# Query tiles by heads on the row halves: a recurrent-memory attention kernel on one Trainium2 core

## The chip, the cores and the metric

The kernel runs on one core of one Trainium2 chip. The metric is the device time in microseconds, the median of several runs. The engines are TensorE (PE, with its weight loads listed apart as PEld), VectorE (DVE), ScalarE (ACT), GpSimd (POOL) and SyncE (SP, which here only issues DMAs). ACT and POOL can issue DMAs too, each from its own queue. TensorE writes to PSUM, eight banks of 2 KB per partition, and DVE or ACT copy the results to SBUF.

## The reference

Two layers, each a segment-recurrent attention with memory followed by a gated feed-forward, both behind a layer norm and with a residual. The sequence has 2048 rows of 448, cut into 64 segments of 32; 8 memory rows go ahead of each segment, so L = 40.

```python
for s in range(n_seg):
    h = jnp.concatenate([mem, xs], axis=1)
    q = jnp.einsum('btd,dhe->bhte', h, Wq)
    k = jnp.einsum('btd,dhe->bhte', h, Wk)
    v = jnp.einsum('btd,dhe->bhte', h, Wv)
    scores = jnp.einsum('bhqe,bhke->bhqk', q, k) * scale
    scores = jnp.where(mask[None, None], scores, -1000000000.0)
    p = _softmax(scores, axis=-1)
    o = jnp.einsum('bhqk,bhke->bhqe', p, v)
    o = jnp.einsum('bhte,hed->btd', o, Wo)
    mem = o[:, :M, :].copy()
    outs.append(o[:, M:, :])
...
x = x + _A_ref(_layernorm(x), ...)
x = x + _B_ref(_layernorm(x), ...)
x = x + _A_ref(_layernorm(x), ...)
x = x + _B_ref(_layernorm(x), ...)
```

There are 16 heads of 256. `_B_ref` is `(relu(x Wg) * (x Wu)) Wd` with an inner width of 1792. The same weights serve both layers.

## The kernel before, in words

**Folding.** The kernel never forms q, k or v. For each head it prepares A = Wq Wk^T (448 x 448) and B = Wv Wo (448 x 448) once, from the weights. Then scores are (h A) h^T, and the output is the sum over heads of (p h) B. Dimension 448 is held in four chunks: three of 128 (kd 0 to 2) and a last one of 64 (kd 3). Heads go in pairs (index eo), four pairs (p4) make a half (hf), and there are two halves.

**Preparation, the A loop** (lines 374 to 409, eight head pairs p). `load_nat` (line 302) loads a pair's columns of Wq and Wk into one of six `nat` buffers by three DMAs on SP's queue; the 64 last rows lie in chunk 3, and the upper 64 partitions of it hold other rows (Wv's last rows beside Wk's). `flips` (line 323) transposes them on TensorE, 16 transposes for Wq and 16 for Wk, and copies the results to `qT`, `kT` and (Wv's last rows) `v3`. A unit of the loop is one (kd, eo): two products of 384 columns into an `aps` bank and two of 64 columns into `mx_ps`. `share` (line 316) gives each copy from PSUM to DVE or ACT, whichever a small model of the two expects to be done first. The flips of the next pair are put between the units (line 400). For kd = 3 only 64 of the 128 rows exist in A_sb, and the copies (lines 394 to 399) put some tiles on the lower and some on the upper 64 partitions, as the table `EARLY` wants it.

**Preparation, the B loop** (lines 411 to 437). Per pair six units of two products of 448 columns (`bps`), then a group of four half-width products (`v3` by `wo`), two on the left and two on the right column half of TensorE. Wv is flipped one pair ahead; Wo comes over POOL's queue, three ahead, each load held back by `spread` until TensorE has reached the place in the program.

**The order of work.** `in_order` chains all of TensorE's instructions in program order. `InOrder` does so for DVE and ACT, but only once `on` is set (line 1037), that is after the preparation; during it the compiler's scheduler may order the two engines' work. `bank` picks the PSUM bank that is free first by a running estimate. `keep_warm` issues products of zeros that nobody reads: eight ahead of the first transposes, four between the flips of the first Wq and the first Wk.

**The scan** (line 1039). 68 steps; two chains run side by side, the two layers, the second four segments behind the first, so eight steps have one chain and 60 have two. Every other step also holds a feed-forward block. In a step `project` multiplies A by the rows (tiles of 128 columns, collected in banks of up to six tiles as `BANKS` orders them) and the copies fill `TQ` (tiles 0 to 23) and `TZ` (tiles 24 to 27, the 64 last dimensions). `project_early` does the kd 3 part of two banks at once, on the two row halves of TensorE. `scores` multiplies `TQ` and `TZ` by the rows, chunk by chunk in the order `KD`: for the second half, all memory and own scores of the first three chunks of `KD`, then those of the last chunk. `weigh_m` and `weigh_x` multiply the transposed weights `PT` by the rows, and `project_out` multiplies by B.

**Where things lie, before.** Tile t of a half holds chunk kd = t // 8, head parity eo = t // 4 % 2, pair p4 = t % 4, and TQ's columns are in the order of the tiles. So the last bank (tiles 18 to 23) belongs to chunk 2, and the bank before it (12 to 17) finishes chunk 1.

Of the kernel before, what the change touches and what calls it, by code (L numbers as in the profile page):

```python
# [15 lines left out]
DM = 448  # L16
# [26 lines left out]
EARLY = (((0, 6), (12, 18)), ((0, 6), (12, 18)))  # L43


KD = (0, 1, 3, 2)
# [4 lines left out]
def upper(hf, t):  # L51

    return any(b <= t < b + 6 for _, b in EARLY[hf])


def tidx(kd, eo, p4):

    return kd * 8 + eo * 4 + p4 if kd < 3 else 24 + p4


def build_kernel(ctx, tc, A_x, A_mem0, A_Wq, A_Wk, A_Wv, A_Wo, B_W_gate, B_W_up, B_W_down, out,
# [31 lines left out]
    class InOrder:  # L93

        def __init__(self, eng):
            self.eng, self.last, self.on = eng, None, False

        def __getattr__(self, name):
            f = getattr(self.eng, name)

            def call(*a, **k):
                r = f(*a, **k)  # L102
                if self.on:
                    if self.last is not None:
                        tc.add_manual_dep(r.ins, self.last,
                                          mybir.DependencyInfo(mybir.DependencyClass.NoSync,
                                                               mybir.DependencyReason.DATA),
                                          reason="order of issue")
                    self.last = r.ins.name
                return r  # L110

            return call
# [55 lines left out]
    nc.sync.dma_start(xp[1][:], x_dram[0:128])  # L168
# [120 lines left out]
    with tc.tile_pool(name="pre", bufs=6) as pre:  # L289
# [3 lines left out]
        nats = []  # L293
        for i in range(6):
            t = pre.tile([P, 4, 512], BF, name=f"nat{i}", bufs=1)
            nats.append(t)
        nc.gpsimd.memset(A_sb[64:128, 3, :, 24:NT, :], 0.0)
        for t in TQ + TZ + PX + PM + YB:
            nc.gpsimd.memset(t[:], 0.0)
        nn = [0]  # L300

        def load_nat(src, p, eng):
            t = nats[nn[0] % 6]
            nn[0] += 1
            cols = slice(512 * p, 512 * (p + 1))
            eng.dma_start(t[:, 0:3, :], src[0:384, cols].rearrange("(k p) n -> p k n", p=P))
            if src is Wv:
                return t
            eng.dma_start(t[0:64, 3, :], src[384:448, cols])
            eng.dma_start(t[64:128, 3, :], (Wq if src is Wq else Wv)[384:448, cols])  # L310
            return t

# [3 lines left out]
        def share(dst, src, n, per):  # L316
            cost = {dve: 60 + n * per[0], act: 170 + n * per[1]}
            ends = {e: max(until[e], now[0]) + cost[e] for e in cost}
            eng = min(ends, key=ends.get)
            until[eng] = ends[eng]  # L320
            evac(eng, dst, src)

        def flips(src, p, name):
            nat = load_nat(src, p, nc.sync)
            o = pre.tile([P, 4, 512], BF, tag="tT", name=name, bufs=4)

            def half(e2):
                tp = bank([P, 2, 512], BF, "tpw")
                n = 3 if src is Wv else 4
                for kd in range(n):  # L330
                    for e in range(2):
                        tr(tp[:, e, kd * 128:(kd + 1) * 128],
                           nat[:, kd, (2 * e2 + e) * 128:(2 * e2 + e + 1) * 128], ident[:])
                n = DM if src is Wk else 128 * n
                share(o[:, 2 * e2:2 * e2 + 2, 0:n], tp[:, :, 0:n], 2 * n, (0.6, 0.82))
                if src is Wk:
                    share(v3[:, p, 2 * e2:2 * e2 + 2, :], tp[:, :, DM:512], 128, (0.6, 0.82))

            return o, [lambda: half(0), lambda: half(1)]

        def queue(p):
            if p < NP:
                qT, a = flips(Wq, p, "qT")
                kT, b = flips(Wk, p, "kT")
                return (qT, kT), a + b
            if p == NP:
                return flips(Wv, 0, "vT")
            return None, []
# [13 lines left out]
        keep_warm(8)  # L362
# [5 lines left out]

        ready, todo = queue(0)
        for k, u in enumerate(todo):  # L370
            if k == 2:
                keep_warm(4)
            u()
        for p in range(NP):
            hf, p4 = divmod(p, 4)
            qT, kT = ready
            ready, todo = queue(p + 1)
            mx_ps = bank([P, 4, 128], F32, "mxw")
            for kd in range(4):
                for eo in range(2):  # L380
                    aps = bank([P, 3, 128], F32, "aps")
                    for t in range(2):
                        e = 2 * eo + t
                        mm(aps[:, :, :], qT[:, e, kd * 128:(kd + 1) * 128],
                           kT[:, e, 0:384], start=(t == 0), stop=(t == 1))
                    for t in range(2):
                        e = 2 * eo + t
                        mm(mx_ps[:, kd, eo * 64:eo * 64 + 64], qT[:, e, kd * 128:(kd + 1) * 128],
                           kT[:, e, 384:448], start=(t == 0), stop=(t == 1))
                    t0 = eo * 4 + p4  # L390
                    if kd < 3:
                        share(A_sb[:, kd, hf, t0:t0 + 17:8, :], aps[:], 384, (1.28, 0.85))
                    else:
                        up = [t for t in range(3) if upper(hf, t0 + 8 * t)]
                        for rows, ts in ((slice(64, 128), up), (slice(0, 64), [t for t in range(3) if t not in up])):
                            if ts:
                                d = ts[1] - ts[0] if len(ts) > 1 else 1
                                share(A_sb[rows, 3, hf, t0 + 8 * ts[0]:t0 + 8 * ts[-1] + 1:8 * d, :],
                                      aps[rows, ts[0]:ts[-1] + 1:d, :], 128 * len(ts), (1.28, 0.85))
                    if todo and 2 * kd + eo in (0, 2, 4, 5):  # L400
                        todo.pop(0)()
            share(A_sb[:, 0:3, hf, 24 + p4, :], mx_ps[:, 0:3, :], 384, (1.28, 0.85))
            share(A_sb[0:64, 3, hf, 24 + p4, :], mx_ps[0:64, 3, :], 128, (1.28, 0.85))
            if p >= 5:
                load_wo(p - 5)
            if p == 1:
                xn0 = normed(row_stats(xp[1]))
            if p == 2:
                first_rows(xn0)

        for p in range(NP):
            hf, p4 = divmod(p, 4)
            vT = ready
            ready, todo = flips(Wv, p + 1, "vT") if p + 1 < NP else (None, [])
            wo = wos.pop(0)
            for eo in range(2):
                for kd in range(3):
# [6 lines left out]
                    if kd == 1 and todo:  # L424
                        todo.pop(0)()
            bps = bank([P, 512], F32, "bps")
            for t in range(2):
                for eo in range(2):
                    e = 2 * eo + t
                    mm(bps[64 * eo:64 * eo + 64, 0:DM], v3[:, p, e, :], wo[:, e, :],  # L430
                       start=(t == 0), stop=(t == 1), tile_position=(0, 64 * eo))
            share(B_sb[:, hf, 24 + p4, 0:DM], bps[:, 0:DM], DM, (1.28, 0.85))
# [175 lines left out]
    def tile_of(ps, hf, t, i, chains, hb, j, kds, first, last):  # L608

        n = L * len(chains)  # L610
        for kd in kds:
            mm(ps[:, i * n:(i + 1) * n], A_sb[:, kd, hf, t, :], moving(hb, j, kd, chains),
# [518 lines left out]
```

## Time and profile before

| | us |
|---|---|
| median of 3 runs (1569.27 to 1571.19) | 1570.5 |
| the profiled execution | 1569.33 |
| its span | 1567.5 |
| start to the first `aps` product | 9.55 |
| A loop, to the first `bps` product | 38.35 |
| B loop, to the first `prj` product | 27.68 |
| first `prj` product to the end | 1491.9 |

The span is the time from the first to the last instruction; the time of the execution has some 1.8 us around it. The three stretches ahead of the scan end where the first product of the next stage starts in the timeline. Of the work before the scan, the eight loads each of Wq, Wk, Wv and Wo bring 384 to 448 KB apiece, and the 64 last rows of Wq, Wk and Wv come in separate loads of 64 KB.

### The profile page before, as it was taken

To read this page: it belongs to the slowest core of one execution; us is meant where nothing else is said; L and a number is where in the kernel's file an instruction comes from. 1 tells how busy PE (TensorE), PEld (TensorE's weight loads), DVE (VectorE), ACT (ScalarE), POOL (GpSimd) and SP (SyncE) were. 2 spreads that over 40 slices of the span, in tenths; PEclk is the share of its full clock that TensorE was granted. 3 is DMA by queue.
4 is the path that set the end of the run, shared out by engine and by line. 5 is a ranking of instruction groups with operands and counts; after the bars stand their busy time and mean duration, and the time that the engine had idled before them with its cause. 6 is when DMAs were issued, how large, how long until landed. Compare 5 with 4: busy or idle time off the path is not lost.

```text
span 1567.5 us, 89355 instructions
## 1 busy us (share of the span) xinstructions
PE 1554.4 (99%) x40988; PEld 1442.9 (92%) x40988; DVE 1111.4 (71%) x3654; ACT 757.7 (48%) x2123; POOL 78.0 (5%) x174
## 2 busy tenths in 40 slices
PE   9999999999999999999999999999999999999998
PEld 6688999999999999999999999999999999999897
DVE  8756777777767777777677777667777776677765
ACT  5754444454444445544454455444544554445443
POOL 3200000000000000000000000000000000000000
PEclk9999999999999999999999999999999999999999
DMA  8630000000000000000000000000000000000000
GB/s 239 205 86 9 8 10 9 5 8 10 9 10 9 10 10 5 9 9 10 9 10 9 10 3 10 9 10 9 9 10 10 4 9 10 10 8 7 6 7 9
DMA packets 28233, 33.21 MB, mean 21 GB/s; under 512 B 4168, under 2 KB 26960, under 8 KB 27856
## 3 DMA queue, kind: packets, MB, share of 16 engines
q1 hardware_dynamic: 26608, 23.76, 5.4%
q8 instruction: 320, 5.24, 1.4%
q0 software_dynamic: 1088, 3.68, 0.7%
q14 instruction: 57, 0.47, 0.1%
q10 hardware_dynamic: 160, 0.06, 0.0%
HBM read 23.70 MB, written 1.84 MB: 16 GB/s over the span
## 4 chain that ended last, share of the span: by engine, by line
PE 98%; DVE 1%; issue 0%; DMA 0%; SPq 0%; ACT 0%; POOL 0%; POOLq 0%; DVEq 0%; ACTq 0%
PE prj L144 32%; PE ox L144 25%; PE gps L144 6%; PE ups L144 6%; PE dps L144 6%; PE o L144 5%; PE y L144 4%; PE Sx L144 3%; PE pps L152 2%; PE bps L144 1%; PE aps L144 1%; PE Sm L144 1%; PE tpw L152 1%; PE ya L144 1%; PE yb L144 1%; PE tps L152 1%
## 5 line engine op out<-in xcount | busy, mean ns | idle before, releaser
L144 PE MATMUL prj<-hT,A_sb 128*128 128x80 bf16 (+3 forms) x15232 | 550.5, 199 | 2.2 <-issue 1.3
L144 PEld LDWEIGHTS <-A_sb 128*128 128x128 bf16 (+1 forms) x15232 | 504.8, 99 | 22.6 <-issue 3.2
L144 PEld LDWEIGHTS <-B_sb 128*128 128x128 bf16 (+1 forms) x15008 | 489.4, 103 | 13.7 <-issue 0.8
L144 PE MATMUL ox<-Y,B_sb 128*128 128x80 bf16 (+2 forms) x11256 | 443.5, 200 | 1.4 <-issue 1.4
L102 ACT CAST TQ<-prj 128x480 bf16<-128x480 f32 (+1 forms) x380 | 184.1, 497 | 103.1 <-PE prj L144 91.2
L102 DVE CAST Y<-y 128x256 bf16<-128x256 f32 x376 | 151.3, 457 | 39.8 <-PE y L144 39.5
L102 ACT CAST Y<-y 128x512 bf16<-128x512 f32 (+2 forms) x392 | 137.1, 419 | 67.5 <-PE y L144 61.8
L102 ACT ACTIVATE se<-se 128x160 f32<-128x160 f32 (+2 forms) x270 | 81.6, 302 | 138.3 <-DVE se L102 131.8
L102 DVE CAST TQ<-prj 128x480 bf16<-128x480 f32 (+1 forms) x228 | 128.7, 573 | 8.8 <-PE prj L144 8.3
L144 PE MATMUL gps<-xT,Wg_sb 128*128 128x128 bf16 (+3 forms) x1904 | 128.6, 216 | 0.0
L144 PEld LDWEIGHTS <-Wu_sb 128*128 128x128 bf16 (+1 forms) x1904 | 104.9, 97 | 5.6 <-issue 0.2
L102 ACT COPY os<-o 64x16 f32<-64x16 f32 (+3 forms) x134 | 25.5, 191 | 171.7 <-PE o L144 170.1
L144 PE MATMUL ups<-xT,Wu_sb 128*128 128x128 bf16 (+3 forms) x1632 | 106.8, 216 | 0.5 <-DVE xT L102 0.5
L144 PEld LDWEIGHTS <-Wg_sb 128*128 128x128 bf16 (+1 forms) x1904 | 106.7, 97 | 0.5 <-issue 0.5
L144 PEld LDWEIGHTS <-hk 40*128 40x128 bf16 (+1 forms) x1950 | 98.9, 96 | 8.6 <-issue 1.4
L102 DVE SCALAR_TENSOR_TENSOR hh<-gps,ut 128x512 bf16<-128x512 f32 (+2 forms) x136 | 78.1, 595 | 34.6 <-ACT ut L102 21.6
L102 ACT CAST TZ<-prj 64x320 bf16<-64x320 f32 (+2 forms) x264 | 97.0, 377 | 8.2 <-DVE TZ L102 5.3
L144 PE MATMUL dps<-Wd_sb,hh 128*128 128x448 bf16 (+1 forms) x504 | 93.3, 342 | 0.8 <-DVE hh L102 0.8
L102 ACT COPY PT<-pps 128x256 bf16<-128x256 bf16 (+1 forms) x136 | 47.2, 347 | 96.5 <-PE pps L152 92.1
L102 DVE TENSOR_REDUCE ssum<-se 128x4 f32<-128x160 f32 (+2 forms) x270 | 72.9, 270 | 24.1 <-ACT se L102 24.0
L144 PEld LDWEIGHTS <-TQ 128*128 128x128 bf16 x1938 | 85.8, 97 | 1.5 <-ACT TQ L102 0.8
L144 PE MATMUL y<-PT,hk 40*128 40x256 bf16 (+1 forms) x1280 | 86.3, 249 | 0.6 <-ACT Y L102 0.6
(126 smaller groups left out, 1902.3 us busy)
## 6 DMA issues: line engine op xcount, KB each, us to landing
wo<-in_A_Wo_dram POOLq DMA_DIRECT2D x8, 448.0 KB, 5.0
nat<-in_A_Wq_dram SPq DMA_DIRECT2D x8, 384.0 KB, 5.0
nat<-in_A_Wk_dram SPq DMA_DIRECT2D x8, 384.0 KB, 4.9
nat<-in_A_Wv_dram SPq DMA_DIRECT2D x8, 384.0 KB, 4.5
xa<-in_A_x_dram SPq DMA_DIRECT2D x32, 56.0 KB, 2.3
xa<-xp SPq DMA_DIRECT2D x32, 56.0 KB, 1.9
xp<-in_A_x_dram SPq DMA_DIRECT2D x30, 56.0 KB, 2.4
out_dram<-xa SPq DMA_DIRECT2D x30, 56.0 KB, 2.3
```

The source lines that it names most:

```text
L102: r = f(*a, **k)
L144: in_order(nc.tensor.matmul(out, lhsT, rhs, **k))
L152: in_order(nc.tensor.transpose(out, src, idn))
```

## The change

The tiles of the queries are numbered anew. A bank of six tiles now holds one head parity (eo) and six of the twelve (chunk, pair) positions: banks 0 and 6 the positions 0 to 5, banks 12 and 18 the positions 6 to 11. In `A_sb` the kd 3 rows of the even heads lie on partitions 0 to 63 and those of the odd heads on 64 to 127, and `a_tile` turns a tile's number into its place there. In `TQ`, `TZ`, `PT` and the tiles of B the two parities alternate, 16 columns each. Chunk 0 is complete after bank 6; chunks 1 and 2 both need bank 18. `KD` becomes (0, 3, 1, 2), and the second half's scores take the first two chunks, then the other two.

In the preparation, the 64 last rows are loaded apart (`nats3`, Wq's and Wk's side by side, Wv's of two pairs side by side), flipped by four transposes (`flip_last`), and the kd 3 rows of A come from four half-width products of 448 columns (`by_heads`, `last_rows`). The groups of half-width products of two pairs stand next to each other: at the end of an even pair and the start of the odd one. The first loads are cut in two halves of 256 columns, Wq's on SP's and Wk's on ACT's queue; later loads are asked for two pairs ahead and held back by `spread`. Seven idle products instead of eight and four. The first layer norm and the first rows move from the A loop to the B loop, and the first load of x goes behind the first asks. DVE and ACT keep program order from the start.

```diff
-EARLY = (((0, 6), (12, 18)), ((0, 6), (12, 18)))
-KD = (0, 1, 3, 2)
+EARLY = ((0, 6), (12, 18))
+KD = (0, 3, 1, 2)
...
+def a_tile(t):
+    if t >= 24:
+        return t
+    u = t // 12 * 6 + t % 6
+    return 3 * (t // 6 % 2 * 4 + u % 4) + u // 4
 def tidx(kd, eo, p4):
-    return kd * 8 + eo * 4 + p4 if kd < 3 else 24 + p4
+    return kd * 8 + p4 * 2 + eo if kd < 3 else 24 + p4
...
-    nc.sync.dma_start(xp[1][:], x_dram[0:128])
+    nats = [pre.tile([P, 3, 512], BF, name=f"nat{i}", bufs=1) for i in range(6)]
+    nats3 = [pre.tile([P, 512], BF, name=f"natl{i}", bufs=1) for i in range(3)]
+    for e in range(2):
+        cols = slice(256 * e, 256 * e + 256)
+        for i, (eng, src) in enumerate(((nc.sync, Wq), (nc.scalar, Wk))):
+            eng.dma_start(nats[i][:, :, cols], rows3(src, cols))
+            if e == 0:
+                eng.dma_start(nats3[0][FR[i], :], src[384:448, 0:512])
...
+        def ask(p):
+            if p < NP:
+                q, r = load_nat(Wq, p)
+                spread(r)
+                asked[p] = ([q, load_nat(Wk, p)[0]], load_last(((Wq, p), (Wk, p))))
+            elif p < 2 * NP:
+                v, r = load_nat(Wv, p - NP)
+                spread(r)
+                asked[p] = (v, load_last(((Wv, p - NP), (Wv, p - NP + 1))) if p % 2 == 0 else None)
...
+        def flip(nat, e2, dst):
+            tp = bank([P, 2, 512], BF, "tpw")
+            for kd in range(3):
+                for e in range(2):
+                    tr(tp[:, e, kd * 128:(kd + 1) * 128],
+                       nat[:, kd, (2 * e2 + e) * 128:(2 * e2 + e + 1) * 128], ident[:])
+            share(dst, tp[:, :, 0:384], 768, (0.6, 0.82))
+        def flip_last(nat, dst):
+            tp = bank([P, 4, 128], BF, "tpl")
+            for e in range(4):
+                tr(tp[:, e, :], nat[:, e * 128:e * 128 + 128], ident[:])
+            share(dst, tp[:].rearrange("p e (i d) -> p e i d", i=2), 512, (0.6, 0.82))
...
-        keep_warm(8)
+        keep_warm(7)
...
+        def by_heads(ps, a, b, n):
+            for t in range(2):
+                for eo in range(2):
+                    mm(ps[FR[eo], 0:n], a(2 * eo + t), b(2 * eo + t), start=(t == 0), stop=(t == 1),
+                       tile_position=(0, 64 * eo))
+        def last_rows(qk, hf, p4):
+            ps = bank([P, DM], F32, "apl")
+            by_heads(ps, lambda e: qk[:, e, 0, 384:DM], lambda e: qk[:, e, 1, :], DM)
+            eng = one_of(900, (1.28, 0.85))
+            for eo in range(2):
+                t0 = 3 * (eo * 4 + p4)
+                evac(eng, A_sb[FR[eo], 3, hf, t0:t0 + 3, :], ps[FR[eo], 0:384])
+            for eo in range(2):
+                evac(eng, A_sb[FR[eo], 3, hf, 24 + p4, 64 * eo:64 * eo + 64], ps[FR[eo], 384:DM])
         ready, todo = queue(0)
-        for k, u in enumerate(todo):
-            if k == 2:
-                keep_warm(4)
-            u()
+        ask(1)
+        for _ in range(3):
+            todo.pop(0)()
         for p in range(NP):
-            qT, kT = ready
-            ready, todo = queue(p + 1)
+            qk = ready
+            ask(p + 2)
+            ready, us = queue(p + 1)
+            todo += us
+            if p == 0:
+                nc.sync.dma_start(xp[1][:], x_dram[0:128])
+            if p % 2:
+                last_rows(qk, hf, p4)
-            for kd in range(4):
-                for eo in range(2):
+            for eo in range(2):
+                for kd in range(3):
...
+            if p % 2 == 0:
+                last_rows(qk, hf, p4)
...
         for p in range(NP):
             vT = ready
-            ready, todo = flips(Wv, p + 1, "vT") if p + 1 < NP else (None, [])
+            ask(p + 2 + NP)
+            ready, todo = queue_v(p + 1) if p + 1 < NP else (None, [])
+            if p % 2:
+                last_out(p, wo)
...
+            if p % 2 == 0:
+                last_out(p, wo)
+            if p == 1:
+                xn0 = normed(row_stats(xp[1]))
+            if p == 2:
+                first_rows(xn0)
...
-                T = TQ[hf][:].rearrange("p g u w -> p g (u w)")[:, :, 16 * i0:16 * (i0 + k)]
+                u0, eo = i0 // 12 * 6, i0 // 6 % 2
+                T = TQ[hf][:].rearrange("p g u w -> p g (u w)").rearrange("p g (t e q) -> p t e g q", e=2, q=16)
+                T = T[:, u0:u0 + 6, eo]
...
-                mem(KD[:3])
-                own(KD[:3])
-                mem(KD[3:])
-                own(KD[3:])
+                mem(KD[:2])
+                own(KD[:2])
+                mem(KD[2:])
+                own(KD[2:])
...
-                mm(yb[:, 128:192], hk[:, 3 + eo, :], PT[:, 64 * eo:64 * eo + 64], start=(eo == 0), stop=(eo == 1))
+                mm(yb[:, 128:192], hk[:, 3 + eo, :], PT[:].rearrange("p (b o q) -> p b o q", o=2, q=16)[:, :, eo, :], start=(eo == 0), stop=(eo == 1))
...
-                       PT[rows, :].rearrange("p (e o w) -> p e o w", e=2, o=2)[:, :, eo, :],
+                       PT[rows, :].rearrange("p (e b o q) -> p e b o q", e=2, o=2, q=16)[:, :, :, eo, :],
...
-    dve.on = act.on = True
```

`last_out` is the B loop's group of half-width products, by `by_heads` as before.

## The prediction

> **What bounds the kernel now.** First the busy shares and the chain of waits on the page, then the windows cut at the three stages before the scan and the scan itself.
>
> ```profile
> PE 1554.4 (99%) x40988; PEld 1442.9 (92%) x40988; DVE 1111.4 (71%) x3654; ACT 757.7 (48%) x2123; POOL 78.0 (5%) x174
> ...
> PE 98%; DVE 1%; issue 0%; DMA 0%; SPq 0%; ACT 0%; POOL 0%; POOLq 0%; DVEq 0%; ACTq 0%
> ```
> ```profile
> 0.00:9.55 9.55, 7.55 (x45) 4.02 (x46) 4.47 (x20) 1.31 (x2) 8.76 (x17) 1.00 0.69 205
> 9.55:47.90 38.35, 38.35 (x501) 29.81 (x500) 34.69 (x75) 24.64 (x69) 7.30 (x14) 1.00 0.89 265
> 47.90:75.58 27.68, 27.68 (x215) 14.54 (x214) 21.77 (x38) 20.24 (x37) 9.61 (x11) 1.00 0.60 190
> ...
> 116.40:1490.00 1373.60, 1371.02 (x36782) 1293.98 (x36778) 982.86 (x3259) 657.31 (x1801) 48.92 (x124) 1.00 0.03 9
> ```
> After the window's bounds come its length and the busy times of PE, weight loads, DVE, ACT and POOL, then granted clock, DMA share and GB/s. TensorE sets the pace from 9.55 us on: the A loop (9.55 to 47.90), the B loop (to 75.58) and the scan. So an edit is worth what it takes from TensorE's stream, and a new wait costs its full length. In the A loop DVE (34.69) and ACT (24.64) together fill 77% of two engines, and the DMA engines 89%: both covers are thin.
>
> The paces of TensorE come from starts in the timeline, since a product's own duration holds its pipeline's latency.
>
> ```profile
> 10.51 0.49 PE L144 MATMUL aps<-kT,qT 128*128 128x384 bf16 x2
> 10.83 0.22 PE L144 MATMUL mxw<-kT,qT 128*128 128x64 bf16 x2
> ...
> 11.27 0.61 PE L152 MATMUL tpw<-ident,nat 128*128 128x128 bf16 x8
> 11.72 0.49 PE L144 MATMUL aps<-kT,qT 128*128 128x384 bf16 x2
> ```
> ```profile
> 50.46 0.54 PE L144 MATMUL bps<-wo,vT 128*128 128x448 bf16 x2
> 50.93 0.57 PE L144 MATMUL bps<-wo,v 128*64 128x448 bf16 x4
> 51.43 0.93 PE L144 MATMUL bps<-wo,vT 128*128 128x448 bf16 x4
> ```
> A unit of the A loop (two products of 384 columns, two of 64) takes 10.51 to 10.89 = 0.38 us; a transpose 0.45/8 = 0.056 us; two products of 448 columns 0.38 us too (52.54 to 53.67 holds six). The four half-width products of 448 columns start at 50.93 where full ones would end at 50.84, and give way at 51.43: 0.38 us of work, since the two column halves run side by side, and 0.19 us of switching, 0.57 in all.
>
> **The first products.**
>
> ```profile
> 1.18 3.59 PE L144 MATMUL junk<-still 128*128 128x512 bf16 x8 [1.18 <-DVE still L171]
> ...
> 4.92 1.89 PE L152 MATMUL tpw<-ident,nat 128*128 128x128 bf16 x16
> ...
> 6.49 0.26 PEld L144 LDWEIGHTS <-still 128*128 128x128 bf16 x2
> ...
> 9.55 0.49 PE L144 MATMUL aps<-kT,qT 128*128 128x384 bf16 x2 [0.27 <-DVE kT L102]
> ```
> The eighth idle product starts at 4.14, so one takes 0.43 us. The first 16 transposes fill 4.92 to 6.49, 0.098 us each against 0.056 later: TensorE runs at about half pace until some 6.5 us, though the granted clock reads 1.00. Then K's loads hold the rest until 9.55. After the change seven idle products end at 1.18 + 7 x 0.43 = 4.2. The first Q half is issued at about 0.7 in the place of xp, and one such load landed 3.7 us after its issue (1.17 to 4.91), so it is there at 4.4 at the latest. K's half comes over ACT's queue, which may first load its table (0.73 to 2.01). 16 transposes at 0.098 bring 5.8 to 6.0; the last-needed copy of 768 elements (0.56 on DVE, 0.80 on ACT) ends near 6.4, where aps begins: **-3.15 us**. Bounds: 5.8 (everything on DVE, loads early) and 7.5 (table first, 2.0 + 3.7 + 16 transposes), that is -3.75 to -2.05. Half pace may outlast 6.4: each us of it costs 0.5; I take +0.3, bounds 0 and 1.7.
>
> [...]
>
> **Work on TensorE in both loops.** Per head pair the A loop goes from eight units to six: 16 x 0.38 = -6.08 us over eight pairs. Transposes: Q and K 32 to 28 a pair, 16 of them (not 32) before the first unit, V's last rows 4 per two pairs, and the first rows moved from A to B; in the loops 328 before and 328 after: 0. Column-pair groups: eight of 0.57 before (all in B, 4.56); after, eight in A and eight in B, two and two adjacent (end of an even pair, start of the odd one), 2 x 0.38 + 0.19 = 0.95 per two, eight times 0.95 = 7.60: +3.04. Together **-3.04 us**. If adjacent groups switch in between all the same, they cost 16 x 0.57 and this is -1.52.
>
> **Copies.** Per pair, kd 3's four pieces of 64 rows and mxw's (0.26 to 0.43 each, 1.55 together) give way to two of 64x384 and two of 64x64 (1.4, from 0.48 for 384 and about 0.2 for the small ones); Q and K flips get shorter (0.674 and 0.625 to 0.558), v's two of 0.267 go, one of 512 elements (0.44, between 0.265 at 128 and 0.558 at 768) comes. 7.4 us per pair falls to 6.8, and the pair from 4.8 to 2.28 + 28 x 0.056 + 0.475 = 4.32: 79% of two engines. Eight banks cover it on average, not in the burst where two groups of copies (2.8 us) fall together; the odd pair's group also needs the last flip's copy, with 0.38 + 0.48 in between against 0.2 + 0.56 to 0.80. DVE and ACT now keep program order here, so the layer norm's wait for POOL (0.23 + 0.57) holds what is queued behind it. I take +0.8, bounds 0 and 2.5.
>
> **Loads two ahead.** Each ask waits for TensorE's last product at that point and brings 896 KB in four issues. In A the loop lasts 4.3 us; Q is needed 4.7 after the ask and K 5.4, and at the 265 to 300 GB/s of this stage both halves (768 KB, 2.6 to 2.9 us after some 1.8 of issue and latency) are there: 0. In B a V load shares the engines with a Wo load asked at the same time.
>
> ```profile
> DMA to landing us min/median/max: 3.7/4.5/6.1
> ```
> ```profile
> wo<-in_A_Wo_dram POOLq DMA_DIRECT2D x8, 448.0 KB, 5.0
> ```
> The first line is nat in the B loop's window. V is needed 3.54 + 0.38, or 0.86 in odd pairs, after its ask: 4.2 on average. At 4.5 the six loops with a Wo load wait 0.3 each (2.0), at the least row 3.7 nothing. Before, these loads queued behind one another; now each is alone on SP's ring, so I take 1.0, bounds 0 and 3.5. SP's xp and first-rows loads stand behind the asks; the first step needs them 30 us later.
>
> [...]
>
> **The scan.** The count of instructions stays; new tile indices alone, and POOL's zeroing of A_sb in two halves for one of 0.95 us (done by 6, read after 70), cost 0. Scores of half 1 need the last bank's copy for two of four chunks now, not one.
>
> ```profile
> 568.18 0.56 ACT L102 CAST TQ<-prj 128x480 bf16<-128x480 f32 x1 [0.36 <-PE prj L144]
> ...
> 568.52 0.13 PEld L144 LDWEIGHTS <-TQ 128*128 128x128 bf16 x2
> ...
> 568.93 0.21 PEld L144 LDWEIGHTS <-TQ 128*128 128x128 bf16 x5
> ```
> ```profile
> 1544.11 0.42 ACT L102 CAST TQ<-prj 128x48 bf16<-128x48 f32 x2 [0.25 <-PE prj L144]
> ...
> 1544.58 0.14 PEld L144 LDWEIGHTS <-TQ 128*128 128x128 bf16 x3 [0.20 <-ACT TQ L102]
> ```
> The second pair shows a real wait: copy ends 1544.53, load at 1544.58, so 0.05 us to pass on. The copy of the first ends 568.74, free at 568.79. Before, the late chunk comes after 15 products, at 568.94; after, behind 2 of 0.035 and 8 of 0.026, at 568.80. In the other kind of step (copy ending 460.65, first load 460.48) it is 460.76 against 460.70. So the wait just vanishes: 0, and each 0.01 us that the copy is later costs 0.3 to 0.6 us over the 60 steps with two chains. The copies write runs of 16 elements as before, at twice the step: 0. PT is now read as a moving operand in runs of 16. The nearest row is prj, two runs of 40: 67 products in 2.29 us, 34.2 ns for 80 columns, where unbroken operands go at 0.16 us for 384, 33.3 for 80, so a break costs at most 0.9 ns; 60 more breaks a step make at most 54 ns, 3.2 us over the scan. I take 0, the row's break being buried. Nothing gains here, since TensorE waits for nothing.
>
> **The sum.** -3.15 + 0.3 - 3.04 + 0.8 + 1.0 = -4.1 us on the profiled execution's 1569.3 (span 1567.5 and 1.8 around it): 1565.2. The median lies 1.2 above that execution: **1566.4 us**.
>
> **Rivals.** (a) The waits do not come: -3.15 - 3.04 = -6.2, **1564.3**. For: nothing waits in A now. Against: the thinner covers. (b) Loads and copies eat the gain, at their bounds 3.5 + 2.5 with the late half pace 1.7: +1.5, **1572**; half of that excess leaves 1569. For: DMA at 89%. Against: loads fall to 917 KB in 4.3 us, 213 GB/s. (c) The slower side: interleaved TQ writes make the scores of half 1 wait for the last copy at their first load. Place: 568.52 waits for 568.79, 0.27, and 460.48 for 460.70, 0.22; 30 of each are 15 us, **1581**. It decides from 0.068 us a step, which is 4.1 us. For: the ranges of the two head parities now interlace. Against: before, the copies already wrote three-level patterns that spanned all of TQ, and the first load did not wait.
>
> **Chances.** Forecast 0.60, (a) 0.11, (b) 0.16, (c) with smaller forms of the same wait 0.13. About 0.2%, 3.1 us, is what a measurement can tell. The forecast gives 0.47 faster and 0.13 same, (a) 0.11 faster, (b) 0.11 same and 0.05 slower, (c) 0.13 slower: 0.58, 0.24, 0.18. The range reaches from (a) with an early start, 1563, to (b) at its bound, 1572; the forecast's own is 1564 to 1569.
>
> **What would show it.** aps starting near 6.4; the A loop near 35.3 us and the B loop near 29; PEld idle on nat loads in B; no TensorE idle ahead of TQ loads in the scan, whose window from the first prj to the end stays at 1491.9 us. I am wrong if that window moves by more than 2 us, or if the loops together last over 66.

## The result and the profile after

| | before | after |
|---|---|---|
| median of 22 runs each, us | 1569.09 (1567.79 to 1572.14) | 1571.71 (1570.30 to 1576.13) |
| the profiled execution | 1569.33 | 1570.71 |
| its span | 1567.5 | 1568.9 |
| start to the first `aps` product | 9.55 | 6.48 |
| A loop | 38.35 | 39.42 |
| B loop | 27.68 | 32.20 |
| first `prj` product to the end | 1491.9 | 1490.8 |

The ratio after to before is 1.0017 (95% interval 1.0010 to 1.0023): a small loss, where a gain was forecast. The time lies in the range given (1563 to 1572), but the sign is the other one. That it does is in part luck: the three runs that the forecast started from had a median of 1570.5, 1.4 us above that of the 22, so the time is 5.3 us above the forecast, but the change 6.7 (+2.6 where -4.1 was forecast). By stage: the start gained 3.07 us as forecast, the loops, forecast at 35.3 and 29, took 39.42 and 32.20, together far over the 66 that the prediction named as its sign of being wrong, and the scan moved by 1.1.

First the busy times and the chain of waits, shares of the span by engine, on the page of the changed kernel.

```profile
PE 1550.2 (99%) x40935; PEld 1440.1 (92%) x40935; DVE 1108.2 (71%) x3649; ACT 760.6 (48%) x2116; POOL 78.3 (5%) x175
...
PE 97%; DMA 2%; DVE 1%; issue 0%; ACT 0%; POOL 0%; SPq 0%; POOLq 0%; DVEq 0%
```

TensorE is busy for 4.2 us less than before, yet the span is 1.4 longer: the work did go away. What is new is DMA with 2% of the chain. The windows, cut at the same four places (columns as in the prediction), say where:

```profile
0.00:6.48 6.48, 4.87 (x23) 2.48 (x24) 4.18 (x16) 1.65 (x2) 5.67 (x16) 1.00 0.62 171
6.48:45.90 39.42, 35.89 (x448) 26.56 (x448) 29.80 (x64) 27.13 (x63) 9.71 (x14) 1.00 0.72 220
45.90:78.10 32.20, 28.74 (x237) 15.89 (x237) 23.49 (x46) 20.53 (x37) 10.87 (x14) 1.00 0.68 219
116.40:1490.00 1373.60, 1371.97 (x36817) 1295.06 (x36814) 982.65 (x3258) 656.80 (x1796) 48.91 (x124) 1.00 0.03 9
```

The first two figures of a line are its length and PE's busy time. Before, both loops had no gap. Now TensorE stands idle for 39.42 - 35.89 = 3.53 us in A and 32.20 - 28.74 = 3.46 in B; its busy times, 35.89 and 28.74, are close to the 35.3 and 29 forecast for the loops as a whole. Nearly all of it is waits for weight loads (in the order of the loops: total, times, longest):

```profile
PE tpw L154 <- DMA nat<-in_A_Wq_dram: 3.4, 3, 2.4
PE tpw L154 <- DMA nat<-in_A_Wv_dram: 3.5, 3, 2.2
```

The share of the DMA engines in A *fell*, from 0.89 to 0.72: the loads are not too many, they come too late. The chain in order of time (start, length, what) names the loads:

```profile
5.22 5.82 DMA nat<-in_A_Wq_dram
11.09 0.51 PE tpw L154 x6
...
14.79 5.60 DMA nat<-in_A_Wq_dram
20.44 0.51 PE tpw L154 x6
...
24.62 4.85 DMA nat<-in_A_Wq_dram
29.53 0.51 PE tpw L154 x6
...
49.54 4.43 DMA nat<-in_A_Wv_dram
54.02 0.51 PE tpw L154 x6
...
65.85 6.25 DMA nat<-in_A_Wv_dram
72.15 0.51 PE tpw L154 x6
```

Five times the end hangs on a weight load from the moment SP issues it until the transposes that use it: 4.43 to 6.25 us. A pass without waits lasts about 4.5 us in A and 3.6 in B (the busy times over eight). And SP's own queue in the timeline (start, length, issues) shows what stands ahead of two of these five:

```profile
12.43 0.37 SPq L317 DMA_DIRECT2D nat<-in_A_Wk_dram  x1
12.95 0.47 SPq L324 DMA_DIRECT2D natl<-in_A_Wq_dram  x1
13.47 0.59 SPq L324 DMA_DIRECT2D natl<-in_A_Wk_dram  x1
14.16 0.54 SPq L317 DMA_DIRECT2D nat<-in_A_Wk_dram  x1
14.79 1.35 SPq L317 DMA_DIRECT2D nat<-in_A_Wq_dram  x1
...
61.56 1.36 SPq L242 DMA_DIRECT2D Wu_sb<-in_B_W_up_dram  x2
62.97 0.42 SPq L317 DMA_DIRECT2D nat<-in_A_Wv_dram  x1
65.01 0.80 SPq L242 DMA_DIRECT2D Wu_sb<-in_B_W_up_dram  x2
65.85 0.43 SPq L317 DMA_DIRECT2D nat<-in_A_Wv_dram  x1
```

`spread` holds only the Wq load of a pair. The pair's Wk load and last rows are not held, and the compiler issues them first, though the program asks for Wq ahead of them: the load needed first goes last. (Counted through, the last rows and the second Wk load of this fence already belong to the pair after.) In B two held pieces of W_up, asked at the end of the pass before, go ahead of the held Wv load.

The scan shows nothing new. The page has 1.6 us of idle ahead of all 1938 loads of TQ, against 1.5 before (busy, mean ns of one, then the idle ahead and what ended most of it):

```profile
L146 PEld LDWEIGHTS <-TQ 128*128 128x128 bf16 x1938 | 85.7, 97 | 1.6 <-ACT TQ L105 0.9
```

### The profile page after: what moved, and what is told of

The parts are those of the page before. It is cut to its first block, busy times and chain, and to the rows that moved or that the text cites. A ratio compares the mean times of both kernels' runs of the same rounds, so it can differ in the third digit from the quotient of the medians.

```text
span 1568.9 us, 89231 instructions
## 1 busy us (share of the span) xinstructions
PE 1550.2 (99%) x40935; PEld 1440.1 (92%) x40935; DVE 1108.2 (71%) x3649; ACT 760.6 (48%) x2116; POOL 78.3 (5%) x175
## 4 chain that ended last, share of the span: by engine, by line
PE 97%; DMA 2%; DVE 1%; issue 0%; ACT 0%; POOL 0%; SPq 0%; POOLq 0%; DVEq 0%
PE prj L146 32%; PE ox L146 25%; PE gps L146 6%; PE ups L146 6%; PE dps L146 5%; PE o L146 5%; PE y L146 4%; PE Sx L146 3%; PE pps L154 2%; PE Sm L146 1%; DMA nat<-in_A_Wq_dram 1%; PE ya L146 1%; PE bps L146 1%; PE yb L146 1%; PE tps L154 1%; PE kps L146 1%
## 5 line engine op out<-in xcount | busy, mean ns | idle before, releaser
L105 DVE SCALAR_TENSOR_TENSOR hh<-gps,ut 128x512 bf16<-128x512 f32 (+2 forms) x136 | 78.1, 595 | 37.5 <-ACT ut L105 21.7
```

## The experiments

Each was timed against the kernel before on the same chip (the first four against a median of 1569.69 us, the next four 1569.55, the following three 1568.83, the last 1568.47; 15 to 28 runs each). The theory going in: the holding back of loads, and the order on SP that comes with it, cost the gain. The rivals: the copies, the order of VectorE and ScalarE, or the column-pair groups. In the expectations "pair 2" means the second pair (`p` = 1), except in the last one, which counts as the code does, as all of them do for the pieces of W_up and W_gate.

**1. No holds on the weight loads (e1).** The loads go as soon as a buffer is free.

```diff
-                spread(r)        # in ask(), Wq
-                spread(r)        # in ask(), Wv
```

> The changed kernel, but no load of Wq, Wk or Wv is held back by TensorE's progress any more: each goes as soon as its buffer is free. Theory H (holding back makes them late): TensorE's waits for nat loads (4.7 us for Wq and 4.8 us for Wv by the weight-load queue) all but vanish, the A loop falls from 39.4 to about 35.5 us, the B loop from 32.2 to about 28.5, and the time is 6 to 8 us less than the changed kernel's 1571.7, some 1564 to 1566, 0.2 to 0.3% under the kernel before. Rival D (the DMA engines' rate at the start is what is late): the first wait of 2.4 us in the A loop stays, since 1.8 MB have to come before it whoever asks, and only the waits of the B loop go: 1567 to 1569. Rival C (the column-pair groups and the copies are what costs): no change, 1571 to 1572.

Measured: 1565.15 us (11 runs), ratio 0.9973 (0.9964 to 0.9982). Its windows, cut at the same places:

```profile
0.00:6.46 6.46, 5.06 (x23) 2.62 (x24) 4.18 (x16) 1.46 (x2) 5.65 (x16) 1.00 0.60 177
6.46:43.70 37.24, 36.12 (x449) 26.66 (x449) 29.84 (x64) 27.31 (x63) 9.72 (x14) 1.00 0.87 261
43.70:72.20 28.50, 28.21 (x235) 16.18 (x233) 23.33 (x46) 20.48 (x37) 10.81 (x14) 1.00 0.65 208
```

Idle is down to 1.12 and 0.29 us, and the DMA share of A is back at 0.87. The time and B are as theory H had them; A stays above the 35.5 expected, with a wait of 0.77 us for a Wk load at 9.11 in place of the 2.43 for Wq, so a part of the first wait is rival D's. The rest of the change is worth about what the prediction gave it: -4.5 us against the kernel before. Taking the hold away turns the loss into a gain. It also alters SP's queue: in e1 a Wq load goes ahead of its Wk load again (at 2.48 and 3.01, at 5.82 and 6.53), and the last Wv load (45.3) ahead of the first piece of W_up (59.0). So e1 does not say whether the hold by itself is what makes a load late, or what overtakes it while it is held; the next runs take that apart.

**2. W_up and W_gate pieces asked behind the last Wv loads, holds kept (e2).**

```diff
-            if p >= 3:
-                next_piece()
-                next_piece()
+            if p >= 5:
+                for _ in range(4 if p == 5 else 3):
+                    next_piece()
```

> The changed kernel, but the pieces of Wu and Wg that the B loop asks for (ten, two per pair from pair 3 on) are asked for from pair 5 on (4, 3, 3), so that every load of Wv stands ahead of them on SP's queue. Nothing else moves. If the Wu pieces ahead of the Wv loads cause the two late waits of the B loop (2.17 and 0.81 us), the B loop falls from 32.2 to about 29.2 us, the 0.5 us wait at the third pair stays, and the time falls by about 3 us to 1568.7. If the holding back alone makes Wv late, the B loop keeps its waits and the time stays at 1571 to 1572.

Measured: 1570.55 us (11 runs), ratio 1.0006 (0.9997 to 1.0014). The waits for Wv fall from 4.8 us to 2.6 and B from 32.2 to 30.7: the pieces are a part, not all. (In time e2 and the changed kernel are not told apart, 1.0006 and 1.0017 with intervals that overlap; the windows carry the point.) A, whose code is untouched, took 41.0 in this execution, so single profiles of A differ by 1.6 us.

**3. Only the second pair's Wq load not held (e3).**

```diff
-                spread(r)
+                if p > 1:
+                    spread(r)
```

> The changed kernel, but only the first held-back load (Wq of the second pair) goes at once; all later ones are held back as before. Theory H: that load is issued near 2.5 us ahead of its Wk and lands by 7.5, so the 2.4 us wait in the first pair goes and the A loop is 2 to 2.5 us shorter (37 us), the time 1569.3. Rival D: Wq and Wk of the second pair only change places, the wait moves to Wk, and the gain is under 1 us.

Measured: 1575.26 us (5 runs), ratio 1.0041 (1.0028 to 1.0053): a miss. The wait for Wq at 11 us is gone (0.65 and 0.42 us for Wk are left), but one of 3.87 us appears at 22.65, for a Wq load that SP issued at 15.55 behind two Wk loads, and B takes 32.9. Behind that wait TensorE ran at a granted clock of 0.50 for 3.41 us (the last section tells of it), some 2 us of the loss: A's busy time is 38.04, against 35.89 in the changed kernel. One hold less moves the wait to the next late load.

**4. Column-pair groups apart (e4).** Each at the end of its own pair, in both loops.

```diff
-            if p % 2:
-                last_rows(qk, hf, p4)
...
-            if p % 2 == 0:
-                last_rows(qk, hf, p4)
+            last_rows(qk, hf, p4)
```

> The changed kernel, but every group of column-pair products stands at the end of its own pair, so no two are adjacent. By the sum of the prediction each of the 8 adjacent meetings (4 in A, 4 in B) spares 0.19 us of switching: 1.5 us more than the changed kernel, 1573.2, if nothing hides it. If what waits is the loads, the waits take some of it up and the time rises by less than 1 us; if the bunched copies of two adjacent groups are what costs (rival C), it falls.

Measured: 1572.88 us (9 runs), ratio 1.0027 (1.0017 to 1.0037) against 1.0017 (1.0010 to 1.0023) with the groups adjacent. The intervals overlap; the timeline carries the point. Two adjacent groups in the changed kernel:

```profile
24.02 0.95 PE L146 MATMUL apl<-qk 128*64 128x448 bf16 x8
24.90 0.50 PE L146 MATMUL aps<-qk 128*128 128x384 bf16 x2
```

They are listed at 0.95 us for eight products; alone, in e4 as before, a group of four is listed at 0.57, 1.14 for two. So an adjacency saves 0.19 us, as forecast. Seven of the eight came about, some 1.3 us in all: in B the transposes of the first rows stand between the groups at 56.68 and 57.69. The time of e4 can't show this, since in its profile B ran at a granted clock of 0.50 for 3.41 us (mean over B 0.95).

**5. and 6. SP in program order, with holds (f1) and without (f2).**

```diff
+    sp = InOrder(nc.sync)
-            r = nc.sync.dma_start(t[:], ...)
+            r = sp.dma_start(t[:], ...)
```

The last rows, the first Wq halves, x and the pieces go through `sp` too; f2 also drops the holds of the weight loads.

> The changed kernel with the holds kept, but SP issues its loads of the preparation in the order of the program, so that the Wk and last-rows loads of a pair no longer go ahead of the held Wq load of that pair (in the changed kernel the Wk load of pair 2 went at 2.48 us, the last rows at 3.01 and 4.63, its Wq load only at 5.22). Theory O (being overtaken makes the Wq loads late): the waits of weight loads for Wq of 4.7 us mostly go, the first loop falls from 39.4 us to 36.5-37.5; the second loop keeps some 3 us of waits for Wv, because the pieces of Wu still stand ahead of the Wv loads; time about 1568.7 us, ratio to before 0.9985-1.0000. Theory H (the holding itself is late, whatever the order): Wk and the last rows now wait behind the held Wq load as well, the first loop stays at 39-43 us, time 1571-1574 us, ratio 1.001-1.003.

> The kernel without holds on the weight loads (e1_free, 1565.15 us, ratio 0.9973) with SP's loads of the preparation in program order. If the order on SP costs something also without holds (the one wait of 0.8 us for Wk and 1.2 us for Wq that e1_free still has), the first loop falls from 37.2 us towards 36 and the time to 1564-1564.5 us, ratio 0.9965; if those waits are the DMA engines' share in the first 10 us (0.85 and more), nothing changes: 1565 us, ratio 0.9973 within 0.0008.

Measured: f1 1574.27 us (6 runs), ratio 1.0029 (1.0018 to 1.0041); f2 1570.96 (11 runs), 1.0009 (1.0000 to 1.0017). Both expectations missed in the total, and for one reason. In A theory O came close: f1's loop is 37.8 us, and after 12 us nothing waits for Wq or Wk (a wait of 0.45 at 41.62 is for Wv's last rows). Its window, and the row of the Wq loads in the changed kernel and in f1 (count, KB each, median us to landing):

```profile
6.60:44.40 37.80, 35.66 (x448) 26.48 (x448) 29.99 (x64) 27.34 (x63) 9.61 (x14) 1.00 0.72 224
```
```profile
nat<-in_A_Wq_dram SPq DMA_DIRECT2D x7, 384.0 KB, 4.9
nat<-in_A_Wq_dram SPq DMA_DIRECT2D x7, 384.0 KB, 3.8
```

From the second pass on (issues from 13.76) the five Wq loads of f1 landed in 3.3 to 3.9 us; in the changed kernel those from 14.79 took 3.7 to 5.6. B went to 36.5 in f1 and 35.6 in f2. SP's queue and then TensorE in f2's timeline (in brackets the idle ahead, and what ended it):

```profile
59.02 1.58 SPq L105 DMA_DIRECT2D Wu_sb<-in_B_W_up_dram  x2
60.66 0.42 SPq L105 DMA_DIRECT2D nat<-in_A_Wv_dram  x1
61.12 1.14 SPq L105 DMA_DIRECT2D natl<-in_A_Wv_dram  x2
```
```profile
67.21 0.61 PE L155 MATMUL tpl<-ident,natl 128*128 128x128 bf16 x4 [3.92 <-DMA natl<-in_A_Wv_dram]
```

The Wv loads of f2 are not held, but the W_up pieces ahead of them are; in this queue, kept in order, the held pieces of 59.02 held what stands behind them, to 60.66 and 61.12. In e1 these Wv loads had gone by 45.7, ahead of every piece.

**7. First loads whole, no holds (f3).**

```diff
-    for e in range(2):
-        cols = slice(256 * e, 256 * e + 256)
...
+    for i, (eng, src) in enumerate(((nc.sync, Wq), (nc.scalar, Wk))):
+        eng.dma_start(nats[i][:], rows3(src, slice(0, 512)))
+        eng.dma_start(nats3[0][FR[i], :], src[384:448, 0:512])
```

> e1_free with the first loads of Wq and Wk whole instead of in halves by columns; nothing else changed. Tests the term of the start (first product 9.55 us before, 6.46 in e1_free), of which the prediction gave the halves a part. Theory S (the halves bring the start forward): the first product comes 0.8-2.5 us later, near 7.5-9 us, and the time rises by as much, to 1566-1567.7 us, ratio 0.9978-0.999. Theory N (the start comes from the loads standing first on their queues, with fewer bytes ahead, not from the halves): the first product stays within 0.4 us of 6.46 us, time 1565 us.

Measured: 1566.35 us (11 runs), ratio 0.9977 (0.9968 to 0.9986); the first product at 7.5 us instead of 6.46. Theory S by the place of the first product; in time the two are not told apart. So of the 3.07 us gained at the start some 1.0 is the halves'. The other 2 were not taken apart: loads that stand first on two queues, and fewer transposes and idle products ahead of the first unit.

**8. VectorE and ScalarE in the compiler's order during the preparation, no holds (f4).**

```diff
-            self.eng, self.last = eng, None
+            self.eng, self.last, self.on = eng, None, False
...
+                if not self.on:
+                    return r
...
+    dve.on = act.on = True
```

> e1_free with the order of VectorE's and ScalarE's work left to the compiler until the scan, as in the kernel before (the changed kernel issues them in program order from the first instruction). The prediction put the copies' bursts at +0.8 us (0 to 2.5) and did not name the order by itself. If the program's order makes copies wait, the loops fall by 0.5-2 us together: 1563.2-1564.7 us, ratio 0.996-0.997; if it costs nothing, the time stays within 0.7 us of e1_free's 1565.15; if the compiler's own order is the worse one, it rises above 1566 us.

Measured: 1572.23 us (11 runs), ratio 1.0015 (1.0007 to 1.0024), far above the 1566 that the last branch named. VectorE and then TensorE in its timeline:

```profile
14.39 0.63 DVE L105 BATCH_NORM_STATS2 stats<-xp 128x6 f32<-128x448 bf16 x1 [7.27 <-DMA xp<-in_A_x_dram]
```
```profile
16.19 0.80 PE L148 MATMUL aps<-qk 128*128 128x384 bf16 x2 [6.22 <-DVE qk L105]
```

The compiler puts the first layer norm ahead of the copies, as it may; x no longer loads first, so VectorE waits 7.27 us for it, with the copies behind, and TensorE 6.22. The A loop takes 45.4 us, 10.24 of them at a granted clock of 0.50 from 11.4 on (mean over A 0.89). Program order on these two engines, to which the prediction gave no price of its own, is what makes the later load of x harmless: some 7 us (1572.23 against 1565.15; 1.0015 and 0.9973 of the kernel before), of which the half clock is a part.

**9. and 10. f1 and f2 with the pieces behind the Wv loads (g1, g2),** by the edit of experiment 2.

> f1_sp_order (holds kept, SP in program order) with the pieces of Wu and Wg asked from pair 5 of the second loop on, behind the last Wv loads. f1 had the first loop at 37.6 us and the second at 36.5, with 7.0 us of waits for last rows of Wv, 4.5 of them at 70.12, behind four pieces of Wu issued from 61.80 on. Theory Q (what is late is a load that stands behind others on SP's queue; holding by itself costs little): the second loop falls to 29-31 us, the waits for Wv to under 2 us, the time to 1566.5-1569 us, ratio 0.998-0.9995. Theory H (a held load is issued too late in any order): the second loop stays above 33 us and the time above 1571 us.

> f2_free_order (no holds on the weight loads, SP in program order) with the pieces of Wu and Wg asked from pair 5 of the second loop on. f2 had 35.6 us in the second loop with one wait of 4.4 us for last rows of Wv, issued behind two pieces of Wu at 59.02. Theory Q: that wait goes, the second loop comes to 28.5-30 us as in e1_free (28.5), the time to 1564-1566 us, ratio 0.9965-0.998. If program order costs something else in the second loop, it stays above 32 us and the time above 1568 us.

Measured: g1 1569.55 us (11 runs), ratio 1.0006 (0.9997 to 1.0015); g2 1564.77 (10 runs), 0.9977 (0.9967 to 0.9986). g2 is as theory Q had it: B falls from 35.6 to 28.6 us by the pieces' place alone. The windows of B in f2 and in g2 show how:

```profile
43.65:79.22 35.57, 31.35 (x235) 17.54 (x234) 23.36 (x46) 20.60 (x37) 10.89 (x14) 0.90 0.54 168
43.64:72.19 28.55, 28.25 (x235) 16.21 (x234) 23.35 (x46) 20.50 (x37) 10.81 (x14) 1.00 0.64 198
```

3.9 us of the 7.0 are idle, and 3.1 are busy time, at a mean clock of 0.90 against 1.00: the half clock behind the wait. g1 is neither theory's: B is 32.7, with three waits of 1.90, 1.17 and 1.89 us for last rows of Wv and no piece ahead of them. There the pair's last rows stand behind its own held Wv load, as SP's queue and the weight loads in g1's timeline show:

```profile
40.71 4.72 SPq L105 DMA_DIRECT2D nat<-in_A_Wv_dram  x2
45.48 1.13 SPq L105 DMA_DIRECT2D natl<-in_A_Wv_dram  x2
```
```profile
50.79 0.24 PEld L155 LDWEIGHTS <-natl 128*128 128x128 bf16 x4 [1.90 <-DMA natl<-in_A_Wv_dram]
```

The first of the two is issued at 45.48, they are wanted at 48.89 and the second is there at 50.79: 3.4 us of lead where 5.3 were needed, with no piece in the way.

**11. and 12. Holds kept, loads asked three pairs ahead: at once (g3), and from the second pass on (g4).** The diff is g3's; g4 has no `ask(2)` ahead of the loop, and asks for 2 in the first pass, 3 and 4 in the second, then `p + 3`.

```diff
         ask(1)
+        ask(2)
...
-            ask(p + 2)
+            ask(p + 3)
...
-            ask(p + 2 + NP)
+            ask(p + 3 + NP)
```

> The changed kernel with loads asked three pairs ahead instead of two, holds kept, SP's order left to the compiler. Theory Q (being overtaken on SP by Wk and last rows, and by Wu): a pass more of lead, some 4.3 us in the first loop and 3.5 in the second, covers waits of 0.2-2.5 us; the first loop falls to 37-38 us, the second to 28.5-30, the time to 1565-1567.5 us, ratio 0.9975-0.9985. If the waits come from the DMA engines' load rather than from the moment of issue, the first loop stays at 39 us or more, since as many bytes lie ahead: 1570-1573 us.

> The changed kernel with loads asked three pairs ahead from pair 1 on (pair 2 in the first pass, pairs 3 and 4 in the second), holds kept, SP's order left to the compiler. With three pairs asked from the start (g3_three_ahead) one wait of 8.9 us for Wq stood at 15.37, while all later loads were in time: 37.5 us from there to the end of the first loop, 28.6 in the second. Theory Q (a held load that others overtake needs a pass more of lead): the first wait falls back to 2-3 us, the loops take 37.5-39 and 28.5-29 us, time 1565-1567 us, ratio 0.9965-0.9985. If the burst of loads is what makes the first one late, wherever the burst stands, a wait of 4 us or more appears in the second or third pass and the time stays above 1570 us.

Measured: g3 1573.80 us (6 runs), ratio 1.0031 (1.0019 to 1.0044); g4 1566.76 (11 runs), 0.9987 (0.9978 to 0.9996), the time as expected and the ratio just above. In both, B has no wait for Wv and lasts 28.6 us, with W_up pieces still ahead of Wv loads and SP's order left alone; in A nothing waits after 22 us. So a pass more of lead covers the hold and what overtakes it, in both loops, once the first pass is over. What g3 loses is the start: with three pairs asked at once the second pair's Wq load lands at 15.3, a wait of 8.74 us. g4 keeps the first wait of 2.72, and the A loop is 40.4 us, above the 37.5 to 39 expected, for a second reason, told in the last section.

## Why the prediction was wrong

**The start: right.** -3.15 forecast, -3.07 measured, `aps` at 6.48 against 6.4. Half pace, +0.3, was of the right kind: in the changed kernel the first unit goes at full pace (6.48 to 6.87), in e1 its two long products take 0.60 us instead of 0.33. No run shows the 0.3 or its bound of 1.7 as such; they were the author's estimates. Measured were 0 in the changed kernel and 0.27 us in e1, whose next two long products take 0.32 again (7.79 to 8.11).

**Work on TensorE: about right.** Without waits for Wq, Wk or Wv the loops take 36.0 us (A in f3) and 28.55 (B in e1), for 35.3 forecast in A and, without the 1.0 of waits, 28 in B. One of the eight adjacencies did not come about. (The two lengths that the prediction named, 64.3 together, are some 0.5 us less than its terms make of the 66.03 before, 64.8.)

**Copies: over-priced.** The sum took +0.8. In A after, one wait of 0.44 us came in the place that the prediction named: the first two adjacent groups last 13.91 to 15.23, 1.32 us instead of 0.88, and the second group's weight load goes at 14.76, behind the copy that ends at 14.70. In B, e1 has one of 0.29. But the order of VectorE and ScalarE belonged into the sum as a condition: without it +7 (f4).

**The scan: right.** Rival (c) did not come. The scan's 1490.8 us against 1491.9 lie within what the scans of the twelve runs above differ by (1489.9 to 1492.2).

**Loads two ahead: the step that failed.** It gave A 0 and B 1.0; TensorE waited 3.4 and 3.5 us for these loads, 5.9 more. Three parts of it were wrong.
- *The order on SP.* "Each ask waits ... and brings 896 KB in four issues" took all four as held and in the program's order. By the diff only one is held, and it goes last. f1 puts it first: idle in A falls from 3.53 to 37.80 - 35.66 = 2.14 us, and the load lands in 3.3 to 3.9 us. So "2.6 to 2.9 us after some 1.8", at most 4.7, was enough for a load that goes first (no run shows the 1.8 apart; it was the author's estimate); behind Wk and last rows the same load took 5.60 (14.79) and 4.85 (24.62).
- *The first pass.* There Wq, issued at 5.22, is wanted at 8.66, while the first pair's last half lands only at 7.72: it took 5.82 us, and in order (f1, issued at 4.38) still 5.37. The row of the kernel before already held such times, though for loads that queue behind one another:

```profile
nat<-in_A_Wq_dram SPq DMA_DIRECT2D x8, 384.0 KB, 5.0
```
- *What a held load is moved past.* In B the sum named the Wo load on the engines but not the W_up pieces on SP. e2 puts them at about 1.5 us in B; g2 against f2 shows 7.0, half clock included, where order is kept and the pieces are held. The row that the 1.0 was worked out from (3.7/4.5/6.1) is not B's either: of its eight Wv loads, issued from 35.2 to 50.7, only the last was issued in B, and it landed in 3.7.

In A the order alone (f1) or a pass more of lead with the order left as it is (g4) ends the waits for Wq and Wk behind the first ones, but for 0.2 us. In B neither the order with the pieces moved (g1, 32.7) nor the pieces moved alone (e2, 30.7) is enough; a pass more of lead (g4, 28.6) or no hold (e1, 28.5) is. So in B the short lead of a held load is the root, and what overtakes it or stands behind it sets the size; in A, the first pass aside, it hurts only together with the overtaking. How the idle in A divides between the two to better than 1 us is open, since single profiles of A differ by 1.6.

Rival (b) named the direction (loads at their bound, 3.5 us, with the copies at theirs) and missed the place: it looked for shared bandwidth, and the DMA engines had room, since e1 has them at 0.87 in A with nearly all loads in time. That its 1572 lies next to the measured 1571.71 is luck: most of its 2.5 us for copies and its 1.7 of half pace did not come, and the base was 1.4 too high.

e1 and g2 are both faster than either kernel (0.9973 and 0.9977 of the time before); e1 is the smaller edit.

## What to carry to other kernels

A load that is held back until a place in the program needs as lead its time to landing together with everything that will stand ahead of it on its queue: here the same 384 KB took 3.3 to 3.9 us where they went first (f1) and up to 6.25 where they did not (the changed kernel). If one pass is not clearly more than that, ask another pass ahead or do not hold the load. In f2's queue, kept in order, a held piece held what stood behind it (a wait of 3.92 us); in the changed kernel's, left to the compiler, the Wk load at 12.43 went ahead of the held Wq load, at 14.79: read the queue's own timeline before pricing it. And when a load moves back, look for whatever engine may now run its user early and wait there with other work behind (in f4 VectorE, 7.27 us).

## What the runs showed of the hardware beyond that

In g4 a gap of TensorE cost more than its length. After the wait of 2.72 us the granted clock is 0.50, in a window of g4 and in TensorE's timeline:

```profile
12.00:13.00 1.00, 1.00 (x9) 0.65 (x8) 0.56 (x1) 0.26 (x1) 1.00 (x1) 0.50 0.86 214
```
```profile
11.24 0.82 PE L154 MATMUL tpw<-ident,nat 128*128 128x128 bf16 x6 [2.72 <-DMA nat<-in_A_Wq_dram]
11.86 0.84 PE L146 MATMUL aps<-qk 128*128 128x384 bf16 x2
```

(The third figure from the end of the window is the clock, 0.50.) The six transposes start at 11.24 and the next product 0.62 us later; in the changed kernel, at 11.09 and after a wait of 2.43 us, it was 0.35, at a clock of 1.00. Full clock returns at 14.5 (the mean is 0.50 from 13 to 14 us and 0.87 from 14 to 16). By the busy times of A, 37.35 us against 35.89 in the changed kernel, the gap cost another 1.5 us; in g3, after 8.74 us, 2.3 (38.15).

The length of the gap alone did not decide it. One execution of e4 has both kinds (two waits in TensorE's timeline, and a window behind the second):

```profile
11.33 0.51 PE L154 MATMUL tpw<-ident,nat 128*128 128x128 bf16 x6 [2.59 <-DMA nat<-in_A_Wq_dram]
68.27 0.62 PE L154 MATMUL tpw<-ident,nat 128*128 128x128 bf16 x6 [2.16 <-DMA nat<-in_A_Wv_dram]
```
```profile
69.00:71.00 2.00, 2.00 (x11) 1.25 (x10) 0.62 (x1) 1.30 (x2) 0.66 (x2) 0.50 0.85 271
```

The longer gap left the clock at 1.00 (10 to 14 us); after the shorter one it was 0.50 from 68.5 to 71.9. In the loops the clock of 0.50 behind a gap lasted 3.41 us in e3, e4, f1 and g4, 6.83 in f2 and 10.24 in f4 and g3, with a mean over the loop of 0.95 in B of e4 and f1, 0.90 in B of f2, 0.96 in A of g4 and 0.89 in A of f4 and g3 (e3: 0.50 from 24 to 26 us, 0.64 on average from 26 to 28). No run moved a gap on purpose: what sets whether the clock falls, and for how long, was not shown.
